# Attention and two MoE layers on one core: K, Q and V loads earlier in the plan, and the row maximum subtracted on VectorE

## The chip, the cores and the metric

One core of one Trainium2 chip runs the whole program in one launch. The metric is the device time of a run in microseconds (us). Engines are named as the profile names them: PE is TensorE (PEld its weight loads), DVE is VectorE, ACT is ScalarE, POOL is GpSimd, SP is SyncE, which here only issues DMAs (its rows read SPq).

## What is computed

Chunked attention over 4 batches, 8 heads, 768 positions and head size 64, and then two dense layers over the 3072 tokens, each with a hidden width of 2048:

```python
for c in range(24):                       # chunks of 32 queries
    k_full = concat(mem_k, k[c*32-16 : c*32+40])   # 8 memory rows, 56 of the window
    v_full = concat(mem_v, v[the same rows])
    scores = scale * q_c @ k_full.T
    scores = scores - max(scores, axis=-1)
    a = exp(scores); a = a / (sum(a) + 1e-9)
    out[c] = a @ v_full
x = out as (3072, 512)
h = x @ w_in;  x = (max(h, 0) + alpha * min(h, 0)) @ w_out          # layer 1
h = x @ w2_in; x = (h / (1 + exp(-1.702 * h))) @ w2_out              # layer 2
```

## The kernel before

The tokens are cut into 12 blocks of 256, numbered `nb` 0 to 11. A product in high precision is made of several fp16 ones: an operand is scaled by a power of two (found from its absolute maximum) and split into a high and a low fp16 half. Layer 1 runs 96 steps (12 blocks by 8 slices of the hidden width), each with 24 matmuls for the first product (line 585, `h`) and 24 for the second (line 667, `acc`) some steps later. Layer 2 follows from about 705 us on and touches nothing of the change.

The attention of block `nb` has to be ready before layer 1 reaches that block, so its pieces are strewn between the steps of earlier blocks. A table `ATT` gives each piece a due time in thirds of a step; for blocks 3 to 11 the due time is 24 nb - 26 plus the table's number, and blocks 0 to 2 have entries of their own in a second table, `start`. The pieces in the order of use:

- `att_load` (line 302) issues the loads of Q (`qf`, line 307) or of K or V (`kf`, `vf`, lines 319 to 323) on SP. There is one buffer of each, so a load waits until the block before has been split. For blocks at the start or end of a batch a small memset on POOL (lines 313, 315) goes ahead of the load.
- `att_max` (line 332) takes the absolute maxima of K and Q on ACT (V's on DVE); `att_all` brings them over all partitions with three small matmuls (line 120, `mx`), and `att_scale` makes the scales on DVE.
- `att_hi` and `att_lo` (lines 130 and 133) split K, Q and V; this frees `kf`, `qf` and `vf`.
- `att_tk` and `att_tq` (lines 459, 445) transpose K and Q by DMA; `att_swap` (lines 451, 452) copies the transposed Q into a second tile with its halves exchanged. All are issued on SP.
- `att_vw` and `att_vr` bring V into its banded layout through DRAM.
- `att_qk` (lines 483, 484) makes the scores of half a block in PSUM (`sps`), `att_ext` (lines 498, 500) copies the band out of it on ACT. There is one `sps`, so `att_qk` of the second half waits for `att_ext` of the first.
- `att_smax` (lines 514, 515) takes the row maximum on DVE and subtracts it; `eng(nb)` is VectorE for block 0 and GpSimd for the others. `att_exp` (line 519, ACT), `att_sum` (lines 524 to 528, the last on `eng(nb)`), `att_a16`, a DMA transpose and `att_pv` (line 553) follow.

The slices of layer 1's weights (line 154 or 156 loads one of 1 MB) and those of layer 2 are loaded, scaled and split in the same stretch. At the end of a block `y_evac` copies the result out of PSUM (line 706, or 697 for the first blocks), which frees the banks for the next block's second product.

An order is made from this plan: the pieces are recorded by due time, and a scheduler then lays each engine's instructions in a row by when it thinks that their inputs are there. Each engine works through its own row strictly, so an instruction that waits holds up all that stand behind it. SP's row is one row of this kind: all loads, transposes and stores stand in it.

Of the kernel before, what the change touches and what calls it, by code (L numbers as in the profile page):

```python
# [14 lines left out]
ALU = mybir.AluOpType  # L15
# [22 lines left out]
def kernel(  # L38
# [14 lines left out]
    nc = tc.nc  # L53
    B, H, S, D = q.shape
# [9 lines left out]
    SL = WIN + NM  # L64
# [220 lines left out]
    def eng(nb):  # L285
        return nc.vector if nb == 0 else nc.gpsimd
# [221 lines left out]
    def spare(nb, i, a):  # L508
        return att["sx", nb, i][:, a + 1:a + H + 1].rearrange("p (h t) -> p h t", t=1)

    def att_smax(nb, i):
        sc = att["s", nb, i]
        mx = spare(nb, i, 0)
        nc.vector.tensor_reduce(out=mx, in_=sc, axis=AX.X, op=ALU.max)
        eng(nb).tensor_tensor(out=sc, in0=sc, in1=mx.to_broadcast([128, H, SL]), op=ALU.subtract)

    def att_exp(nb, i):
        sc = att["s", nb, i]
# [320 lines left out]
    def run_plan(t):  # L839
# [6 lines left out]
    EX3 = 3 * EX  # L846

    ATT = [
        (-7, att_load, 1), (-6, att_load, 0), (-5, att_load, 2),
        (0, att_max, 1), (1, att_max, 0), (1, att_max, 2), (2, att_all, 0, 3), (4, att_scale, 0, 3),  # L850
        (5, att_hi, 1), (6, att_lo, 1), (6, att_hi, 0), (8, att_tk), (7, att_lo, 0), (9, att_tq),
        (14, att_hi, 2), (15, att_lo, 2), (16, att_vw), (13, att_swap),
        *[(17 + h // 2, att_vr, h) for h in range(H)],
        (18, att_qk, 0), (18, att_ext, 0), (20, att_smax, 0), (21, att_qk, 1), (21, att_ext, 1),
        (22, att_exp, 0), (23, att_smax, 1), (24, att_sum, 0), (25, att_exp, 1), (26, att_a16, 0),
        (27, att_sum, 1), (28, att_ta, 0), (29, att_a16, 1), (31, att_ta, 1),
        (32, att_pv, 0), (33, att_xhi, 0), (34, att_xlo, 0), (34, att_pv, 1), (35, att_xhi, 1), (36, att_xlo, 1),
# [5 lines left out]
    def split(m, p):  # L863
# [6 lines left out]
        (-89.08, alpha_prep), (-85.94, att_qk32, 0, 0), (-84.86, w_load, 0, 0), (-82.33, att_v32, 0, 1),  # L870
        (-78.47, w_load, 1, 0), (-74.28, w_max, 0, 0), (-68.89, att_ext, 0, 0), (-58.71, att_qk32, 0, 1),
        (-54.62, att_ext, 0, 1), (-47.58, att_smax, 0, 0), (-45.32, att_exp, 0, 0), (-41.66, att_sum, 0, 0),
        (-34.37, w_all, 0, 0, 1), (-33.6, w_max, 0, 1), (-31.58, w_scale, 0, 0, 1), (-28.74, att_v32, 0, 0),
        (-28.07, att_load, 1, 1), (-27.6, att_smax, 0, 1), (-26.72, w_all, 0, 1, 2), (-25.47, att_exp, 0, 1),
# [220 lines left out]
```

## Time and profile before

| | us |
|---|---|
| runs before (3) | 1183.9, 1180.58, 1184.12; median 1183.9 |
| the profiled execution | 1185.11 |
| its span | 1183.3 |
| PE busy | 1067.3 (90%) |
| DVE busy | 837.6 (71%) |
| ACT busy | 629.9 (53%) |
| POOL busy | 621.3 (53%) |

The span is the time between the first and the last instruction; 1.8 us of the execution lie outside it. Three stages can be told apart: up to about 225 us the weights and the first blocks are made ready, from 225 to 660 us layer 1 runs beside the attention of blocks 4 to 11, and from 660 us on PE has hardly a gap. PE's busy time does not say whether it runs at full speed, so the granted clock of a stretch is read beside it (1.00 is 2.4 GHz, 0.50 is 1.2 GHz). A row in a timeline that ends in brackets names the idle time of that engine ahead of the instruction and what ended it.

### The profile page before, as it was taken

The numbers are of one execution on the slowest core, as the hardware profiler recorded it, in microseconds if no ns is written. First come the engines' busy times: TensorE is split into PE (matmuls) and PEld (weight loads), VectorE is DVE, ScalarE is ACT, GpSimd is POOL, SyncE is SP. The second block draws the span as 40 slices with busy tenths as digits, with TensorE's granted clock in tenths as the row PEclk, the third lists the DMA queues.
The fourth block names the chain that finished last, engine by engine and source line by source line (L and its number), as shares of the span: only waits on it lengthen the run. The fifth ranks groups of instructions, "written<-read, shape, count | busy, mean of one in ns | idle before, by whom it ended". The sixth has DMA issues, their size and how long they took to land.

```text
span 1183.3 us, 25481 instructions
## 1 busy us (share of the span) xinstructions
PE 1067.3 (90%) x10231; PEld 944.5 (80%) x10231; DVE 837.6 (71%) x1512; ACT 629.9 (53%) x965; POOL 621.3 (53%) x737
## 2 busy tenths in 40 slices
PE   4667888998997989898989999989999999999998
PEld 3655677987886879687878888878888888888887
DVE  6898995768767685858687444887676767667662
ACT  4557455566757476646666533454454444443442
POOL 2245440228565365607563702778676666665672
PEclk9878888999999999998999999999999999999999
DMA  9968228568997777877975480640200202000001
GB/s 215 307 127 195 81 78 171 95 146 204 248 210 221 163 194 166 222 135 201 190 199 134 123 326 19 268 170 19 75 25 6 77 19 81 19 6 14 19 19 37
DMA packets 250534, 154.50 MB, mean 131 GB/s; under 512 B 201200, under 2 KB 221680, under 8 KB 249392
## 3 DMA queue, kind: packets, MB, share of 16 engines
q1 hardware_dynamic: 250416, 152.88, 49.9%
q8 instruction: 80, 1.31, 0.5%
q14 instruction: 38, 0.31, 0.1%
HBM read 91.96 MB, written 38.93 MB: 111 GB/s over the span
## 4 chain that ended last, share of the span: by engine, by line
PE 44%; DVE 20%; DMA 11%; POOL 9%; issue 9%; ACT 5%; SPq 3%; ACTq 0%; POOLq 0%; DVEq 0%
PE acc L681 17%; PE x L596 16%; PE acc L667 5%; PE h L585 4%; DVE g L133 2%; DVE wmax L127 2%; POOL wh L242 2%; DVE wr L201 2%; DVE wr L202 2%; DVE h L625 2%; POOL ga L632 2%; DMA wbig<-in_moe_w_in_dram 2%; POOL yh L767 1%; DMA q<-q 1%; DVE wr L208 1%
## 5 line engine op out<-in xcount | busy, mean ns | idle before, releaser
L632 POOL TENSOR_TENSOR ga<-ga 128x128 f32<-128x128 f32 x384 | 213.1, 579 | 171.0 <-DVE ga L630 158.9
L667 PE MATMUL acc<-g,wbig 128*128 128x256 f16 x2304 | 284.7, 283 | 18.8 <-ACT yf L706 9.4
L585 PE MATMUL h<-xt,wbig 128*128 128x256 f16 x2304 | 274.7, 276 | 19.7 <-DVE g L133 7.4
L667 PEld LDWEIGHTS <-wbig 128*128 128x128 f16 x2304 | 231.8, 101 | 54.0 <-issue 20.6
L585 PEld LDWEIGHTS <-wbig 128*128 128x128 f16 x2304 | 226.8, 99 | 50.0 <-issue 22.0
L681 PE MATMUL acc<-w2o,g 128*128 128x256 f16 x2016 | 230.3, 273 | 4.5 <-ACT g L130 3.8
L596 PE MATMUL x<-yt,w2i 128*128 128x256 f16 x2016 | 229.8, 273 | 2.1 <-DVE ha L606 2.1
L681 PEld LDWEIGHTS <-g 128*128 128x128 f16 x2016 | 196.8, 98 | 28.9 <-ACT g L130 4.7
L596 PEld LDWEIGHTS <-w2i 128*128 128x128 f16 x2016 | 197.2, 98 | 25.2 <-issue 2.4
L133 DVE SCALAR_TENSOR_TENSOR g<-ga,gk,g 128x896 f16<-128x896 f32 x96 | 120.8, 1265 | 91.3 <-ACT g L130 90.9
L130 ACT ACTIVATE g<-ga,gk 128x896 f16<-128x896 f32 x96 | 99.0, 1038 | 95.9 <-POOL ga L632 87.0
L625 DVE SCALAR_TENSOR_TENSOR h<-t,oma,h 128x256 f32<-128x256 f32 x176 | 84.9, 482 | 49.2 <-ACT t L622 47.7
L133 DVE SCALAR_TENSOR_TENSOR g<-h,gk,g 128x512 f16<-128x512 f32 x84 | 62.6, 746 | 61.2 <-ACT g L130 60.7
L130 ACT ACTIVATE g<-h,gk 128x512 f16<-128x512 f32 x84 | 57.5, 685 | 77.2 <-DVE h L625 75.0
L815 POOL TENSOR_TENSOR o<-o 128x256 f32<-128x256 f32 x77 | 74.3, 979 | 10.0 <-ACT o L810 9.5
L629 ACT ACTIVATE ga<-ha,l2t 128x512 f32<-128x512 f32 x48 | 34.5, 718 | 80.6 <-DVE ha L608 80.6
L622 ACT ACTIVATE t<-h 128x512 f32<-128x512 f32 x96 | 56.7, 590 | 33.1 <-PE h L585 24.1
L217 POOL TENSOR_TENSOR wbig<-wr,wbig 128x1024 f16<-128x1024 f32 x16 | 37.4, 2344 | 49.0 <-ACT wbig L212 49.0
L231 POOL TENSOR_TENSOR wt<-wr 128x512 f32<-128x512 f32 x16 | 23.0, 1440 | 74.2 <-DVE wr L208 74.2
L500 ACT COPY sc<-sps 32x504 f32<-32x504 f32 (+2 forms) x112 | 56.2, 502 | 1.0
L242 POOL TENSOR_TENSOR wh<-wt,wh 128x512 f16<-128x512 f32 x32 | 41.6, 1304 | 18.8 <-ACT wh L241 18.8
L630 DVE SCALAR_TENSOR_TENSOR ga<-ga,ha 128x512 f32<-128x512 f32 x48 | 35.6, 741 | 21.1 <-ACT ga L629 21.0
(196 smaller groups left out, 1460.5 us busy)
## 6 DMA issues: line engine op xcount, KB each, us to landing
yt_dr<-yh SPq DMA_DIRECT2D x42, 256.0 KB
yt<-yt_dr SPq DMA_DIRECT2D x42, 256.0 KB
w<-in_moe_w_in_dram SPq DMA_DIRECT2D x10, 1024.0 KB
w<-in_moe_w_out_dram SPq DMA_DIRECT2D x10, 1024.0 KB
vbd<-v_dr SPq DMA_DIRECT2D x80, 112.0 KB
w2i_dr<-wh SPq DMA_DIRECT2D x28, 256.0 KB
w2o_dr<-wh SPq DMA_DIRECT2D x28, 256.0 KB
w2i<-w2i_dr SPq DMA_DIRECT2D x4, 1792.0 KB
```

The source lines that it names most:

```text
L130: return nc.scalar.activation(out=hi, in_=src, func=ACTF.Copy, scale=s)
L133: return nc.vector.scalar_tensor_tensor(out=lo, in0=src, scalar=s, in1=hi, op0=ALU.mult, op1=ALU.subtract)
L242: nc.gpsimd.tensor_tensor(out=hv[:, 1], in0=src, in1=hv[:, 0], op=ALU.subtract)
L500: nc.scalar.copy(d[32 * c:32 * c + 32, ..., 0:WIN], x[32 * c:32 * c + 32, ..., bo + CH * c:bo + CH * c + WIN])
L585: nc.tensor.matmul(out=hp[:, e], lhsT=w[:, wt, o:o + 128], rhs=x[:, xh, kk], start=(n == 0), stop=(n == 3 * KT - 1))
L596: nc.tensor.matmul(out=xs[bank][:, i], lhsT=w[:, o, wt, kk * 256 + c:kk * 256 + c + 128], rhs=yt[sb, yi][:, yh, kk], start=(n == 0), stop= ...
L622: nc.scalar.activation(out=t, in_=hp, func=ACTF.Relu, scale=-1.0)
L625: nc.vector.scalar_tensor_tensor(out=g[:, e], in0=t[:, e], scalar=oma[:, f:f + 1], in1=hp[:, e], op0=ALU.mult, op1=ALU.add)
L632: nc.gpsimd.tensor_tensor(out=g[:, out_], in0=g[:, x], in1=g[:, y], op=op)
L667: nc.tensor.matmul(out=acc[layer, b][dt // 2][:, dt % 2 * TB:(dt % 2 + 1) * TB], lhsT=w[:, wt, dt * 128:(dt + 1) * 128], rhs=g16[:, gh, e] ...
L681: nc.tensor.matmul(out=acc[layer, b][bank][:, i * 256:(i + 1) * 256], lhsT=g16[:, gh, gs], rhs=w[:, o, wt, p % 2], start=(p == 0 and n == ...
L815: e.tensor_tensor(out=ov[:, out_], in0=ov[:, x], in1=ov[:, y], op=op)
```

## The change

Two lines change. The subtraction of the row maximum goes to VectorE for all blocks. And in the table, the loads of a block move forward against the rest: K from -7 to -16.6, Q from -6 to -16.3 and V from -5 to -8.

```diff
--- before.py
+++ after.py
@@ -512,7 +512,7 @@
         sc = att["s", nb, i]
         mx = spare(nb, i, 0)
         nc.vector.tensor_reduce(out=mx, in_=sc, axis=AX.X, op=ALU.max)
-        eng(nb).tensor_tensor(out=sc, in0=sc, in1=mx.to_broadcast([128, H, SL]), op=ALU.subtract)
+        nc.vector.tensor_tensor(out=sc, in0=sc, in1=mx.to_broadcast([128, H, SL]), op=ALU.subtract)
 
     def att_exp(nb, i):
         sc = att["s", nb, i]
@@ -846,7 +846,7 @@
     EX3 = 3 * EX
 
     ATT = [
-        (-7, att_load, 1), (-6, att_load, 0), (-5, att_load, 2),
+        (-16.6, att_load, 1), (-16.3, att_load, 0), (-8, att_load, 2),
         (0, att_max, 1), (1, att_max, 0), (1, att_max, 2), (2, att_all, 0, 3), (4, att_scale, 0, 3),
         (5, att_hi, 1), (6, att_lo, 1), (6, att_hi, 0), (8, att_tk), (7, att_lo, 0), (9, att_tq),
         (14, att_hi, 2), (15, att_lo, 2), (16, att_vw), (13, att_swap),
```

Since two blocks lie 24 units apart, -16.6 and -16.3 for one block are 7.4 and 7.7 on the scale of the block before it: behind that block's split of K (5 and 6) and about its split of Q (6 and 7), and in front of its transposes (8 and 9). For V, -8 is 16 there, right behind the split of V (14 and 15). The rows of all engines come out anew, for the scheduler sees other times.

SP, the block whose K is transposed at about 504 us (`k_6355` is its split K, `q_6492` its transposed Q, `kf` and `qf` take the next block's K and Q), before:

```order
L459 DMA_TRANSPOSE kt<-k_6355 128x8x128 x2
L243 DMA w2i_dr_103<-wh 128x2x512
L459 DMA_TRANSPOSE kt<-k_6355 128x8x48
L445 DMA_TRANSPOSE q_6492<-q_6368 128x16x128
L319 DMA kf<-in_k_dram 120x8x64
L319 DMA kf<-in_k_dram 128x8x64
L319 DMA kf<-in_k_dram 32x8x64
L451 DMA q_6627<-q_6492 64x2048
L452 DMA q_6627<-q_6492 64x2048
L320 DMA kf<-in_mem_k_dram 8x8x64
L323 DMA kf<-in_mem_k_dram 8x8x64
L307 DMA qf<-in_q_dram 128x8x64 x2
```

The same place now (`q_6499` is the transposed Q):

```order
L319 DMA kf<-in_k_dram 120x8x64
L319 DMA kf<-in_k_dram 128x8x64
L319 DMA kf<-in_k_dram 32x8x64
L243 DMA w2i_dr_103<-wh 128x2x512
L320 DMA kf<-in_mem_k_dram 8x8x64
L323 DMA kf<-in_mem_k_dram 8x8x64
L307 DMA qf<-in_q_dram 128x8x64 x2
L459 DMA_TRANSPOSE kt<-k_6355 128x8x128 x2
L459 DMA_TRANSPOSE kt<-k_6355 128x8x48
L445 DMA_TRANSPOSE q_6499<-q_6368 128x16x128
L451 DMA q_6634<-q_6499 64x2048
L452 DMA q_6634<-q_6499 64x2048
```

All seven loads now stand ahead of the transposes; before, three stood between the transposes and the swap, and four behind the swap. On PE the distance is what it was: between the three matmuls of `att_all` and `att_qk` of the first half there are five groups of 24 matmuls of each product, before and now.

DVE at about 99 to 109 us (`xt` is block 1's attention output, `wmax` the maxima of weight slices, `gf` layer 1's activation, `sc` block 2's scores), before:

```order
L133 SCALAR_TENSOR_TENSOR xt<-xp,blk_133,xt 128x4x128 x2
L127 TENSOR_REDUCE wmax_113<-wbig 128x1
L625 SCALAR_TENSOR_TENSOR gf<-t,oma,h 128x256 x2
L514 TENSOR_REDUCE sc<-sc 128x8
L127 TENSOR_REDUCE wmax_114<-wbig 128x1
L625 SCALAR_TENSOR_TENSOR gf<-t,oma,h 128x256 x2
L524 TENSOR_REDUCE sc<-sc 128x8
```

And now:

```order
L133 SCALAR_TENSOR_TENSOR xt<-xp,blk_133,xt 128x4x128 x2
L127 TENSOR_REDUCE wmax_113<-wbig 128x1
L201 TENSOR_SCALAR wr<-wr 128x1024
L625 SCALAR_TENSOR_TENSOR gf<-t,oma,h 128x256 x2
L202 SCALAR_TENSOR_TENSOR wr<-wbig,wr 128x1024
L208 SCALAR_TENSOR_TENSOR wr<-wbig,wr 128x1024
L514 TENSOR_REDUCE sc<-sc 128x8
L625 SCALAR_TENSOR_TENSOR gf<-t,oma,h 128x256 x2
L515 TENSOR_TENSOR sc<-sc 128x512
L127 TENSOR_REDUCE blk_135<-vf 128x1
L625 SCALAR_TENSOR_TENSOR gf<-t,oma,h 128x256 x2
L524 TENSOR_REDUCE sc<-sc 128x8
```

The subtraction (L515) is in DVE's row, two places behind its maximum (L514), and the maximum of a slice of the second weight (`wmax_114`) is gone from between L514 and L524; it now stands 30 rows after L514.

SP from about 115 to 154 us, the difference in one piece (`aT` is block 2's transposed attention weights, `w` and `wbig` are slices of layer 1's second weight):

```order
 L474 DMA vbd<-v_dr_91 56x8x128
 L475 DMA vbd<-v_dr_91 8x8x128
+L156 DMA wbig<-in_moe_w_out_dram 128x2x512
 L540 DMA_TRANSPOSE aT<-a_1104 128x8x128
+L540 DMA_TRANSPOSE aT<-a_1173 128x8x128
 L156 DMA w_526<-in_moe_w_out_dram 128x2x512
-L540 DMA_TRANSPOSE aT<-a_1173 128x8x128
 L156 DMA w_654<-in_moe_w_out_dram 128x2x512
 L156 DMA wbig<-in_moe_w_out_dram 128x2x512
```

A weight load that stood 20 rows ahead of this place is now the first of it, and the transposition of the second half of block 2 stands ahead of a weight load that was in front of it. POOL's row loses its 22 subtractions and keeps the rest nearly in order.

## Rows read from the trace of the kernel before

**Rows 1.** stretch; busy us (instructions) of PE, PEld, DVE, ACT, POOL; clock, DMA

```profile
225.00:660.00 435.00, 388.97 (x4137) 344.55 (x4135) 317.19 (x592) 271.36 (x428) 224.82 (x192) 0.98 0.77 184
...
660.00:1184.00 524.00, 511.62 (x4750) 456.82 (x4747) 336.93 (x564) 231.48 (x336) 316.38 (x487) 1.00 0.21 73
```

**Rows 2.** what TensorE waited for, 225 to 660 us: total, times, longest us

```profile
PE sps L483 <- ACT sc L500: 17.3, 6, 6.5
...
PE acc L667 <- ACT yf L706: 9.4, 6, 3.1
...
PE h L585 <- DVE g L133: 7.4, 7, 1.9
```

**Rows 3.** line 332 (absolute maxima, ScalarE): idle time before it, times, by releaser

```profile
  DMA qf<-in_q_dram: 39.5, 9
...
  DMA kf<-in_mem_k_dram: 5.8, 1
```

**Rows 4.** timeline of ScalarE, 512 to 537 us: start, us, what [idle before]

```profile
522.77 1.48 ACT L332 ACTIVATE junk<-kf 128x1536 f16<-128x1536 f32 x1 [9.26 <-DMA qf<-in_q_dram]
...
533.81 2.32 ACT L500 COPY sc<-sps 32x504 f32<-32x504 f32 x4
```

**Rows 5.** timeline of TensorE, same block

```profile
523.19 0.23 PE L483 MATMUL sps<-kt,q 128*128 128x160 f16 x1
...
536.18 0.29 PE L483 MATMUL sps<-kt,q 128*128 128x160 f16 x1 [6.48 <-ACT sc L500]
```

**Rows 6.** timeline of TensorE, two other blocks

```profile
246.69 3.07 PE L667 MATMUL acc<-g,wbig 128*128 128x256 f16 x24 [1.44 <-DVE yf L697]
...
312.39 0.23 PE L483 MATMUL sps<-kt,q 128*128 128x160 f16 x1 [0.95 <-ACT sc L500]
```

**Rows 7.** timeline of VectorE (first row) and SyncE's queue, same block

```profile
502.62 1.82 DVE L133 SCALAR_TENSOR_TENSOR k<-kf,blk,k 128x1536 f16<-128x1536 f32 x1 [0.99 <-ACT k L130]
...
504.50 2.62 SPq L459 DMA_TRANSPOSE kt<-k  x2
...
509.35 1.94 SPq L445 DMA_TRANSPOSE q<-q  x1
...
511.34 3.52 SPq L319 DMA_DIRECT2D kf<-in_k_dram  x3
...
514.97 0.47 SPq L451 DMA_DIRECT2D q<-q  x1
...
517.75 1.33 SPq L307 DMA_DIRECT2D qf<-in_q_dram  x2
```

**Rows 8.** busy time and granted clock after that stall, columns of rows 1

```profile
534.20:541.00 6.80, 4.82 (x29) 4.00 (x29) 4.52 (x7) 5.73 (x11) 6.80 (x7) 0.50 0.86 179
```

**Rows 9.** chain of work that ended last: start us, us, what

```profile
193.98 6.73 DMA q<-q
...
341.85 4.49 DMA q<-q
```

**Rows 10.** line 515 on both engines (ns min/median/max), and ScalarE waiting for it

```profile
L515 POOL TENSOR_TENSOR sc<-sc x22: 1034/1044/1508, 45.5 to 657.0; 128x512 f32<-128x512 f32 x22
...
L515 DVE TENSOR_TENSOR sc<-sc x2: 675/676/677, 19.6 to 31.5; 128x512 f32<-128x512 f32 x2
...
ACT sc L519 <- POOL sc L515: 8.4, 9, 3.9
```

**Rows 11.** line 133 on VectorE, a form with both inputs in SBUF

```profile
L133 DVE SCALAR_TENSOR_TENSOR g<-gf,gka,g x5: 736/739/2610, 116.6 to 132.2; 128x512 f16<-128x512 f32 x5
```

**Rows 12.** timelines of VectorE, TensorE, SyncE, TensorE between 100 and 201 us

```profile
106.05 1.22 DVE L127 TENSOR_REDUCE wmax<-wbig 128x1 f32<-128x1024 f32 x1 [3.84 <-DMA wbig<-in_moe_w_out_dram]
...
134.55 1.44 PE L553 MATMUL sps<-aT,vbd 128*128 128x32 f16 x48 [4.79 <-DMA aT<-a]
...
128.04 0.41 SPq L156 DMA_DIRECT2D w<-in_moe_w_out_dram  x1
...
200.85 0.29 PE L484 MATMUL sps<-kt,q 128*128 128x160 f16 x1 [4.39 <-DMA q<-q]
```

## Prediction

> **What bounds the kernel now.** I read the busy time by stretch first. From 660 us on TensorE works 511.6 of 524 us at a granted clock of 1.00 [rows 1]; the change touches nothing there, and this half of the time stays. From 225 to 660 us TensorE works 389.0 of 435 us, at 0.98, while VectorE works 317.2, ScalarE 271.4 and GpSimd 224.8 [rows 1]: no helper is full, so the 46 us in which TensorE stands still come from waits, not from an engine that has too much to do. Ahead of 225 us VectorE is close to full, and a fault on its row is passed on.
>
> The list of TensorE's waits says which. The largest, 17.3 us in six pieces, is `att_qk` of a second half (L483) held by ScalarE's copy out of the one `sps` (L500); then 9.4 us of second products behind the evacuation (L706), and 7.4 us of first products behind a split on VectorE [rows 2]. The copy itself is short (2.32 us for the four), so the question is why it comes late. In the block at 512 us ScalarE stood idle for 9.26 us ahead of the absolute maximum of K, until a load had landed, and began the copy only at 533.81 [rows 4]; TensorE had run `att_qk` of the first half at 523.19 and then waited 6.48 us for the second [rows 5]. Over the run that instruction's place on ScalarE costs 39.5 and 5.8 us of idle time, in ten pieces [rows 3]. One block bears this out from the other side: the stall at 312.39 us, in a block with almost no such wait, is 0.95 us [rows 6].
>
> Why the loads are late stands in SyncE's queue: K's split ends at 502.62 + 1.82 = 504.44 us and `kf` is free, but the transposes go first (504.50, 509.35), K's loads are issued from 511.34 and Q's from 517.75 to 519.08, and Q's stand behind the swap (514.97) [rows 7].
>
> **The change part by part.** The sum is made against the profiled execution, 1185.1 us, which is 1.2 us above the median of 1183.9; the result goes back to the median at the end.
>
> *Loads of K and Q, forward.* They are now the first in that queue, from 504.5 us. Seven issues at Q's rate (1.33 us for two, 0.67 each) take 4.7 us; at the durations measured there, 3.52 for three of K, half of the 2.78 us from 514.97 to 517.75 for the two small ones, and 1.33 for Q, they take 6.2 us [rows 7]. So the last is issued by 509.2 to 510.7 us, not 519.1, which is 8 to 10 us earlier, against a wait of 9.26 us at worst: ScalarE's wait should nearly go. What goes with it on TensorE: of the 17.3 us the five pieces other than 312.39 are 16.4 us; if each keeps the 0.95 of the block without a wait, 11.6 go. I take 14, as a stall is not due in every block. With it goes the 1.44 us at 246.69 [rows 6], which follows such a wait. And behind the long stall the granted clock was 0.50 for 6.8 us, in which TensorE worked 4.82 us [rows 8], work that takes half of that at the upper level: 2.4 us. Together **-17.8 us** (11.6 to 20.2).
>
> *What the loads now stand in front of.* The transposes and the swap move back. At 504.5 + 4.7 to 6.2 the transposes start, 4.85 us later (504.50 to 509.35) that of Q is issued, and one such transpose took 4.49 us from issue to landing [rows 7, 9]. The swap is then issued at 518.6 to 520.1 instead of 514.97. How long it takes is seen once where TensorE waited for it: 6.73 us, with loads in the same queue [rows 9]; without them I bound it below by the 4.49 of the transpose. It lands at 523.1 to 526.8, and `att_qk` needs it at 523.19 [rows 5]. That is a stall of 0 to 3.6 us in each of the eight blocks in which the loads overtake the transposes (3 to 10), 0 to 29 us. I take half a microsecond each, **+4 us**, near the lower end, as no load competes with the swap any more.
>
> In the DMA page of the Trainium skill, "DMA: Bandwidth & Descriptors", section "Two DMAs through the same engine are not ordered", descriptors of one queue start in order on each DMA engine though they may end out of order; by that the transposes could not slip past the loads' packets, which speaks for the upper end of this term. The trace agrees in so far as the swap that had loads around it took 6.73 us [rows 9].
>
> *V's loads, forward.* They now stand ahead of the reads of banded V, whose consumer comes some 20 us later in the plan: nothing.
>
> *The subtraction on VectorE.* 22 instructions leave GpSimd at 1.044 us and come to VectorE at 0.676 us [rows 10]: 14.9 us more on VectorE, of which some 10 us lie in the stretch with 435 - 317 = 118 us of idle time. TensorE waits for VectorE in several of its smaller stalls, so I put a quarter on the path, **+4 us** (0 to 15). In return the exponential need not queue behind GpSimd's other work: ScalarE waited 8.4 us for the subtraction, up to 3.9 at once [rows 10], in front of the evacuation that TensorE waits 9.4 us for. I take half of that, **-5 us** (0 to -9.4).
>
> The row for contention: a split with both inputs in SBUF takes 0.739 us at the median and 2.610 at worst [rows 11], and the subtraction has both inputs in SBUF too, so its price lies between 0.68 and 0.68 + 1.87 us. The Trainium skill's page "SBUF — State Buffer", section "Who interferes with whom", says that VectorE with two SBUF inputs and GpSimd reading SBUF shut each other out for a whole instruction; by that the price depends on who starts first, and the subtraction on GpSimd already hit VectorE's splits in the same way.
>
> *The start.* VectorE's 3.84 us wait at 106 us, for a weight that is now loaded and reduced later, goes; TensorE's 4.79 us at 134.55 came from a transpose issued behind a weight load (128.04), which it now precedes; its 4.39 us at 200.85 is a swap like those above, now with loads ahead [rows 12]. Against them stand four subtractions on a full VectorE, 2.7 us, and the weight that comes later. I take **-3 us** (+4 to -10).
>
> Sum: 1185.1 - 17.8 + 4 + 4 - 5 - 3 = 1167.3 us; at the median's level **1166 us**, 1.5% less. The same sum with every part at its good end is 1145, with every part at its bad end 1221; the parts will not all fall one way.
>
> **The rivals.**
> *Late swap (slower).* `att_qk` of each block waits for the swapped Q. If the loads hold the transposes for the full 3.6 us in eight blocks, this costs 29 us: 1185.1 - 17.8 + 29 + 4 - 5 - 3 = 1192, at the median's level 1191. For it: the swap is needed 8.2 us after its issue now (514.97 to 523.19) and comes 3.6 to 5.1 later. Against it: TensorE waited for a swap at only one place after 190 us. It decides from about 2.7 us per block, where eight times the stall eats the other gains of 21.8 us.
> *VectorE shut out.* GpSimd is busy for about half of the stretch [rows 1]; if half of the subtractions meet a reading instruction and wait some 0.9 us (half of 1.87), VectorE gets 14.9 + 10 = 25 us, and with half of it on the path and no gain at the exponential: 1185.1 - 17.8 + 4 + 12.5 - 3 = 1181, median's level 1180. The rule of the Trainium skill's page "SBUF — State Buffer" named above would be its mechanism. Against it: VectorE's idle time.
> *The wait comes back in part.* Small loads or memsets from GpSimd, or a store that stands between the loads, hold SyncE, and ScalarE still waits half as long: half of the first term, 1167.3 + 8.9 = 1176, 1175 at the median's level.
> *It doesn't do what it says.* The new row of ScalarE could bring the maximum forward as far as the loads. Then only the small terms stay: 1182. The order speaks against it.
> *Everything pays.* Late evacuations and half-clock stretches go too: 1148 or less.
>
> **How the numbers follow.** Forecast 0.50; late swap 0.13; VectorE shut out 0.13; half the wait 0.13; nothing 0.05; everything pays 0.06. Faster by over 0.3% (3.6 us, about what a measurement of this kernel can tell from no change) are the forecast, the half wait, the best case and a third of the second rival: 0.73. Within 0.3% are half of that rival and the case of nothing: 0.12. Slower: late swap and the rest, 0.15. The range from 1148 to 1189 reaches the forecast's own bounds and the milder half of the late swap; it leaves out about 0.18.
>
> **What would show it.** Right: line 332 with under 10 us of idle ScalarE time, L483 waiting under 5 us for ScalarE, Q's loads issued ahead of the transposes by 6 us after K's split, and 225 to 660 us shorter by 15 us or more. The swap step is wrong if L483 or L484 waits for the swapped Q in most blocks; the VectorE step if line 515 there takes well over 0.7 us or TensorE's waits for VectorE grow past 10 us; the start if the first 225 us do not shrink. The whole is wrong if ScalarE's wait goes and TensorE's stalls stay, because then something else was due just behind.

## The result: 1169.7 us, 1.0% faster

| | median us | lowest to highest | ratio to before, 95% interval |
|---|---|---|---|
| before | 1183.6 | 1180.6 to 1184.1 | |
| the whole change | 1169.7 | 1167.5 to 1172.4 | 0.9899 (0.9872 to 0.9926) |

Forecast were 1166 us, in a range of 1148 to 1189. The sign and the size fit; the terms are another matter. The traced execution took 1172.38 us with a span of 1170.6, so it is the slowest of these four runs.

To compare two traces, equal work is better than equal time. The cut used from here on is TensorE's row: the *start* ends where the second product (L667) of the third block begins, the *middle* where that of the last block begins. The rest, which is layer 2 but for its first microseconds, takes 482.4 us in both. Of before (from, to, length, busy us of PE, PEld, DVE, ACT and POOL with instructions, granted clock, DMA share, GB/s):

```profile
0.00:221.60 221.60, 163.35 (x1318) 140.10 (x1319) 180.53 (x347) 124.86 (x199) 80.07 (x59) 0.87 0.68 162
221.60:700.90 479.30, 433.27 (x4619) 384.51 (x4616) 337.79 (x641) 291.72 (x459) 241.31 (x206) 0.98 0.77 191
```
And of the whole change:

```profile
0.00:213.60 213.60, 159.21 (x1319) 137.30 (x1320) 175.71 (x347) 123.46 (x197) 72.69 (x51) 0.84 0.69 167
213.60:688.20 474.60, 433.32 (x4615) 384.91 (x4615) 354.00 (x663) 291.61 (x461) 226.51 (x192) 0.97 0.76 194
```
The start is 8.0 us shorter and the middle 4.7. The middle is where the prediction had nearly all of the gain. TensorE's busy time there is the same, 433.3 us, and the granted clock no better (0.97 against 0.98), so what is saved are waits. By name they come to 3.0 of the 4.7 us. What TensorE waited for in the middle, the answer to [rows 2] (us in total, times, longest):

```profile
PE h L585 <- DVE g L133: 9.1, 6, 3.1
PE mx L120 <- DVE g L133: 6.2, 3, 5.3
PE sps L484 <- DMA q<-q: 5.4, 4, 3.0
PE sps L483 <- ACT sc L500: 5.2, 3, 3.0
...
PE acc L667 <- ACT yf L706: 0.9, 1, 0.9
```
L483 behind ScalarE's copy fell from 17.3 us to 5.2, and the second product behind the evacuation (L706) from 9.4 to 0.9. Against these 20.6 us stand 5.4 of a wait that was not there, the swapped Q (L484), and more under VectorE's name: its rows were 17.7 us in all and are 29.8.

SyncE's queue in the block whose K is split at 496.7 us, the answer to [rows 7]:

```profile
496.74 2.91 SPq L319 DMA_DIRECT2D kf<-in_k_dram  x3
...
501.02 1.07 SPq L307 DMA_DIRECT2D qf<-in_q_dram  x2
502.18 5.48 SPq L459 DMA_TRANSPOSE kt<-k  x3
507.71 2.04 SPq L445 DMA_TRANSPOSE q<-q  x1
512.11 0.49 SPq L451 DMA_DIRECT2D q<-q  x1
```
It does what the diff says: K's loads are issued at the split's end, Q's are out at 502.1, 5.4 us after K's first. K's transposes follow at 502.18 instead of at once, Q's at 507.71, and the swap at 512.11. What ScalarE then waits for at line 332 is no load any more, as it was in [rows 3]:

```profile
  DMA q<-q: 17.2, 6
```
```profile
509.59 2.01 ACT L130 ACTIVATE v<-vf,blk 128x1536 f16<-128x1536 f32 x1 [1.85 <-DMA kt<-k]
512.17 1.49 ACT L332 ACTIVATE junk<-kf 128x1536 f16<-128x1536 f32 x1 [0.57 <-DMA q<-q]
```
The scan of K (L332) began at 512.17, just as Q's transpose had landed and the swap could be issued; the split of V ahead of it had itself waited for K's transposes. The reason stands in the code: the scan writes its discarded elements into a buffer of the same tag as Q's split (`q16`), which Q's transpose reads, and V's split goes into the buffer of K's split (`kv16`), which K's transposes read. So the loads came 9 us earlier (5.4 us after the split of K instead of 14.6), the scan only 2.8 (15.5 us after it instead of 18.3), and V's split later. TensorE in that block, the answer to [rows 5]:

```profile
516.68 0.24 PE L484 MATMUL sps<-kt,q 128*128 128x160 f16 x1 [0.80 <-DMA q<-q]
```
The 6.48 us in front of L483 are gone, and 0.80 us for the swap have come.

### The profile page after: what moved, and what is told of

The parts are those of the page before. It is cut to its first block, busy times and chain, and to the rows that moved or that the text cites. A ratio compares the mean times of both kernels' runs of the same rounds, so it can differ in the third digit from the quotient of the medians.

```text
span 1170.6 us, 25487 instructions
## 1 busy us (share of the span) xinstructions
PE 1064.5 (91%) x10231; PEld 942.7 (81%) x10231; DVE 849.6 (73%) x1534; ACT 628.3 (54%) x965; POOL 599.2 (51%) x715
## 4 chain that ended last, share of the span: by engine, by line
PE 48%; DVE 18%; DMA 12%; ACT 6%; SPq 5%; issue 5%; POOL 4%; ACTq 0%; DVEq 0%; POOLq 0%
PE acc L681 17%; PE x L596 16%; PE acc L667 7%; PE h L585 5%; DMA q<-q 2%; SPq L459 2%; DMA w<-in_moe_w_in_dram 2%; DVE g L133 2%; DVE h L625 2%; POOL ga L632 2%; DVE wmax L127 2%; DMA wbig<-in_moe_w_in_dram 1%; DVE wr L202 1%; DMA w<-in_moe_w_out_dram 1%; DVE blk L127 1%
## 5 line engine op out<-in xcount | busy, mean ns | idle before, releaser
L667 PE MATMUL acc<-g,wbig 128*128 128x256 f16 x2304 | 279.5, 280 | 10.9 <-DVE yf L697 4.1
L667 PEld LDWEIGHTS <-wbig 128*128 128x128 f16 x2304 | 230.3, 101 | 43.5 <-issue 11.9
```

Of the source, the lines that this page charges most:

```text
L667: nc.tensor.matmul(out=acc[layer, b][dt // 2][:, dt % 2 * TB:(dt % 2 + 1) * TB], lhsT=w[:, wt, dt * 128:(dt + 1) * 128], rhs=g16[:, gh, e] ...
```

## The experiments

Each group of four ran on one chip beside runs of the kernel before, and is read by its ratio to those. The kernel before had medians of 1182.1, 1179.5 and 1183.3 us on the three chips, so times of different groups are not compared. The ratio is the recorded one and not the quotient of two medians: the loads at -13 have 1172.7 against 1179.5 us, a quotient of 0.9943, near the end of the interval of their 0.9918. Start and middle are from one trace of each kernel, cut as above, and that execution need not be a typical one. The diffs are against the whole change, except where the kernel before is named.

| | ratio, 95% interval | start | middle | TensorE's waits in the middle |
|---|---|---|---|---|
| before | 1 | 221.6 | 479.3 | 45.8 |
| before, second trace | | 217.7 | 479.8 | 44.2 |
| whole change | 0.9899 (0.9872 to 0.9926) | 213.6 | 474.6 | 42.8 |
| whole change, second trace | | 213.5 | 469.6 | 39.0 |
| loads alone | 0.9943 (0.9924 to 0.9961) | 214.3 | 477.4 | 41.8 |
| subtraction alone | 0.9962 (0.9948 to 0.9977) | 213.8 | 483.0 | 47.7 |
| other buffer for the scan | 0.9894 (0.9876 to 0.9912) | 214.7 | 470.8 | 38.9 |
| Q's transpose first | 0.9809 (0.9787 to 0.9831) | 211.9 | 465.4 | 37.6 |
| loads between transposes and swap | 0.9918 (0.9889 to 0.9947) | 213.5 | 475.1 | 40.0 |
| before, Q's transpose first | 1.0051 (1.0033 to 1.0069) | 214.7 | 486.9 | 49.4 |
| loads, Q's transpose first, GpSimd subtracts | 0.9858 (0.9828 to 0.9887) | 213.6 | 465.3 | 34.2 |
| maximum taken twice | 1.0016 (0.9994 to 1.0038) | 221.2 | 475.1 | 42.6 |
| V's loads back at -5 | 0.9950 (0.9929 to 0.9971) | 213.1 | 477.3 | 44.6 |
| Q first and other buffer | 0.9844 (0.9817 to 0.9870) | 211.9 | 472.5 | 40.9 |

### How far one trace can be read

The two kernels once more, unchanged.

> The kernel before, once more with a trace. In the first trace its third block's second product begins at 221.6 us, 7 to 10 us later than in the whole change and in every part of it tried alone. Theory F (the start of before is late because of its order: the swap of block 3 that loads surround, 4.39 us at 200.85, and the half clock behind it): 219 to 223 us again, and 478 to 481 us from there to the last block of layer 1. Rival G (that one execution was late there by chance): under 217 us, and then the gain of 8 us in the start is not the change's.

> The whole change, once more with a trace: the third block's second product at 212 to 215 us and 472 to 477 us from there to the last block of layer 1 if the first trace (213.6 and 474.6) is typical; L483 waits for ScalarE 4 to 7 us, the scan of line 332 for the buffer 15 to 21 us. Otherwise differences of a few us between stages of two traces say nothing.

Before (columns as above):

```profile
0.00:217.70 217.70, 161.65 (x1318) 139.51 (x1319) 180.35 (x347) 124.66 (x199) 80.10 (x59) 0.82 0.67 165
217.70:697.50 479.80, 435.59 (x4620) 386.86 (x4618) 336.96 (x641) 291.74 (x459) 241.24 (x206) 0.97 0.77 191
```
The whole change:

```profile
213.50:683.10 469.60, 431.94 (x4615) 383.75 (x4615) 355.93 (x663) 291.85 (x461) 226.54 (x192) 0.98 0.75 195
```
The start of before ended at 217.7 us and not at 221.6, just under the 219 to 223 of theory F and over the 217 of its rival: about half of the 8 us between the first two traces was one execution's bad luck, and 4.2 us stand between the second two. The middle of before repeats to half a microsecond, that of the whole change differs by 5.0 us, mostly waits (42.8 and 39.0). So from a single trace only differences of 5 us and more in a stage are read here, and the mean of two gives 6.1 us for the start and 7.4 for the middle. Of what was expected of the second trace of the whole change only the start came: its middle is 2.4 us below the 472 expected, L483 waited 3.6 us and line 332 14.2 us for Q's transpose, each just under its range.

### The two halves of the change apart

The loads alone:

```diff
-        nc.vector.tensor_tensor(out=sc, in0=sc, in1=mx.to_broadcast([128, H, SL]), op=ALU.subtract)
+        eng(nb).tensor_tensor(out=sc, in0=sc, in1=mx.to_broadcast([128, H, SL]), op=ALU.subtract)
```

> Only the loads of K, Q and V are moved; the subtraction stays on GpSimd. Theory A (the loads free ScalarE; the subtraction on VectorE is a small net loss, since TensorE's waits for VectorE behind 213.6 us grew by about 12 us while its waits for the evacuation of line 706 fell by 8.5): 1160 to 1168 us, a little faster than the whole change, L483 waiting for ScalarE about 5 us, TensorE's waits for VectorE near the 17.7 us of before, the evacuation near 9 us again. Theory B (the subtraction carries part of the gain): 1173 to 1181 us.

The subtraction alone (the loads back in their old places):

```diff
-        (-16.6, att_load, 1), (-16.3, att_load, 0), (-8, att_load, 2),
+        (-7, att_load, 1), (-6, att_load, 0), (-5, att_load, 2),
```

> Only the subtraction goes to VectorE; the loads stay at -7, -6 and -5. Theory A: 1184 to 1191 us, the waits of line 332 for loads near 45 us and L483 waiting 17 us as before, TensorE's waits for VectorE above 25 us. Theory B: 1173 to 1180 us, with the waits for the evacuation (L706) gone.

Measured were 0.9943 and 0.9962. Theory A falls and B's times fit (1176.0 and 1178.0 us), though the waits for the evacuation did not go with the subtraction alone (5.2 us are left of 9.4): the subtraction is no loss, each half is faster than before, and -0.57% and -0.38% make nearly the -1.01% of both. What TensorE waited for in the middle, loads alone (as [rows 2]):

```profile
PE sps L483 <- ACT sc L500: 3.5, 3, 2.5
```
Subtraction alone:

```profile
PE sps L483 <- ACT sc L500: 16.4, 5, 7.4
```
With the loads alone L483 is down to 3.5 us; with the subtraction alone it stays at 16.4, the middle of its trace is no shorter (483.0 against 479.3 and 479.8), and the gain lies in the start. With the loads alone the middle is 477.4 us, some 2 us shorter, which one trace does not resolve. The rows that name VectorE rise with either half: from 17.7 us in all to 29.8 with the loads alone, where the subtraction is still on GpSimd, to 26.1 with the subtraction alone, and to 29.8 and 25.2 in the two traces of the whole. So this growth is not the price of the subtraction alone. That VectorE's splits are simply due next when TensorE waits less for ScalarE is my reading of it; with the subtraction alone L483 still waits its 16.4 us.

### The buffer of the scan

```diff
-            z = at_p.tile([128, 1536], F16, tag="q16", name="junk")
-            nc.scalar.activation(out=z[:, 0:n], in_=t, func=ACTF.Abs, accum_out=bs(nb, i))
+            z = at_p.tile([128, 1536], mybir.dt.float8e4, tag="a16", name="junk", bufs=2)
+            nc.scalar.activation(out=z[:, 0:n], in_=t, func=ACTF.Abs, accum_out=bs(nb, i), saturate=False)
```

> The whole change, and the scans of K and Q on line 332 write their discarded elements into a buffer of the attention weights (8 bit wide, so that it fits) and not into the buffer of Q's split. Theory A (the 19 us that ScalarE still waits at line 332 are that buffer, which Q's transpose is reading): the wait falls under 5 us, L483's wait for ScalarE from 5.2 to under 3 us, time 1163 to 1169 us. Rival (the wait is a load, or a place on the queue of transposes): the 19 us stay at line 332, time 1168 to 1173 us. Third case: the wait goes and the time stays at 1169, because nothing on TensorE was due behind it any more.

Line 332, idle time by releaser:

```profile
  DMA kf<-in_mem_k_dram: 9.7, 5
```
The 17.2 us behind Q's transpose are gone, so the buffer was their cause; 9.7 us behind K's loads are left, and 1.0 more. And the time is 0.9894, that of the whole change. The third case it is: ScalarE's scan is no longer what TensorE is due on, and removing another wait there buys nothing.

### Q's transpose first

```diff
-        (5, att_hi, 1), (6, att_lo, 1), (6, att_hi, 0), (8, att_tk), (7, att_lo, 0), (9, att_tq),
+        (5, att_hi, 1), (6, att_lo, 1), (6, att_hi, 0), (9, att_tk), (7, att_lo, 0), (8, att_tq),
```

> The whole change, and Q's transpose stands ahead of K's three in the plan (8 and 9 swapped). Theory A (Q's transpose decides both ScalarE's wait at line 332 and the swap): it is issued some 5.5 us earlier, the wait at line 332 falls from 19 to under 6 us, TensorE's waits for the swapped Q (6.7 us in five) go to under 2 us, time 1161 to 1167 us. Rival (K's transposes are then late instead, since first scores need both): TensorE waits for kt by 5 us or more, time 1168 to 1174 us.

1160.9 us, 0.9809: the fastest of all, and at the lower end of what theory A expected. TensorE has no row that waits for `kt`, so the rival falls. SyncE's queue (K's split in this block ends earlier than in the one above):

```profile
493.02 1.01 SPq L307 DMA_DIRECT2D qf<-in_q_dram  x2
494.13 3.42 SPq L445 DMA_TRANSPOSE q<-q  x1
497.65 4.79 SPq L459 DMA_TRANSPOSE kt<-k  x3
502.54 0.53 SPq L451 DMA_DIRECT2D q<-q  x1
```
The swap is issued 8.4 us after Q's transpose, when that had landed (by 500.6 us, when the scan that waited for it began) and K's transposes were out. TensorE's waits in the middle:

```profile
PE h L585 <- DVE g L133: 17.8, 12, 3.0
...
PE sps L484 <- DMA q<-q: 1.8, 1, 1.8
...
PE sps L483 <- ACT sc L500: 0.3, 1, 0.3
```
The swap costs 1.8 us there instead of 5.4 and 3.7 in the two traces of the whole change, and L483 0.3 instead of 5.2 and 3.6. The middle itself:

```profile
211.90:677.30 465.40, 428.73 (x4615) 381.94 (x4615) 349.14 (x663) 290.60 (x462) 233.03 (x193) 0.99 0.80 197
```
TensorE's busy time for the same work is 428.7 us instead of 433.3, at a granted clock of 0.99 instead of 0.97, so less of the middle ran at the lower level. Against the second trace of the whole change the waits are 1.4 us less and the busy time 3.2. One part of the expectation fell: ScalarE still waits 18.5 us at line 332 for Q's transpose, with L483 at 0.3 us.

The same edit on the kernel before tells whether Q first is good by itself:

> The kernel before, with Q's transpose ahead of K's and nothing else. Theory C (Q first gains 9 us on the whole change because it takes back what the loads cost): here there is little to take back, TensorE waits for a swap only once, 4.4 us at 200.85; time 1177 to 1183 us, the waits of line 332 for loads still 40 us or more. Rival D (Q first is good by itself, whatever the loads do): 1168 to 1175 us.

It is not: 1.0051, slower than either theory had it. There the loads of K and Q stand behind the transposes, and L483 waits for ScalarE longer than before:

```profile
PE sps L483 <- ACT sc L500: 22.0, 5, 7.5
```
So of the two places of the loads that were tried with it, Q first pays only with the moved ones. What it takes back there, by the rows, is the late swap and what was left of L483's wait.

### The loads between the transposes and the swap

```diff
-        (-16.6, att_load, 1), (-16.3, att_load, 0), (-8, att_load, 2),
+        (-13, att_load, 1), (-13, att_load, 0), (-8, att_load, 2),
```

> The whole change, but K's and Q's loads at -13 each: in SyncE's row they then stand behind the four transposes and in front of the swap, where SyncE only waits for Q's transpose. Theory C (what the loads cost is the place in front of the transposes: the swap, ScalarE's scan and V's split all wait for transposes that are some 5 us later): the transposes are issued right behind the splits again, VectorE's waits for V's split on ScalarE fall from 10.7 to about 4 us, TensorE's waits for the swap from 6.7 to under 4 us, and the loads come still 5 us sooner than before the change; time 1163 to 1168 us. Rival (the loads themselves have to be that early): ScalarE waits for Q's load at line 332 by over 20 us again, L483 waits for ScalarE over 10 us, time 1171 to 1179 us.

0.9918, 1172.7 us: no better than the whole change. Theory C's signs are there, for in the middle the swap costs 2.9 us and VectorE's wait for V's split 5.2. But the scan waits for K's loads again (over the run):

```profile
  DMA kf<-in_k_dram: 30.4, 7
```
and TensorE's waits under VectorE's name are 30.1 us, no less than in the whole change (29.8 and 25.2). L483:

```profile
PE sps L483 <- ACT sc L500: 5.3, 5, 1.4
```
The rival names the time and the wait for loads at line 332, though for K's loads and not Q's, and misses L483, which stays at 5.3 us. Both places of the loads cost about the same; the later one was not tried with Q's transpose in front.

### The subtraction with Q's transpose first

The loads moved and Q first, but the subtraction on `eng(nb)`:

> Loads moved and Q's transpose first, the subtraction on GpSimd. Theory C (the subtraction on VectorE is worth some 6 us with the loads moved, 1176.0 against 1169.7): 1165 to 1169 us against 1160.9 with the subtraction on VectorE. Rival E (with the late swap gone nothing is due behind the exponential any more, and the subtraction is worth nothing): 1159 to 1163 us.

0.9858 against 0.9809, with intervals that just overlap; 1164.8 us lie between the two forecasts, a little under theory C's. TensorE's waits in the middle show how the two engines differ:

```profile
PE acc L667 <- ACT yf L706: 10.2, 5, 2.5
PE h L585 <- DVE g L133: 9.2, 9, 2.3
```
The middle is the same to 0.1 us (465.3 and 465.4). With GpSimd the second products wait 10.2 us behind the evacuation and the first 9.2 behind VectorE; with VectorE it is 2.3 and 17.8. In these two traces the engine of the subtraction only decides under which name TensorE waits. But the traced executions took 1163.1 and 1161.5 us, 1.6 us apart, where the two ratios are 0.5%, some 6 us, apart. So the traces hold only a part of the difference, and that the subtraction is worth nothing in the middle is not shown.

### More work on VectorE

```diff
         nc.vector.tensor_reduce(out=mx, in_=sc, axis=AX.X, op=ALU.max)
+        nc.vector.tensor_reduce(out=mx, in_=sc, axis=AX.X, op=ALU.max)
```

> The whole change, with the row maximum of line 514 taken twice on VectorE: 24 instructions of 0.68 us, 16.3 us more on VectorE and on the way to the exponential. If a quarter of VectorE's time is on the path, as the prediction had it for the subtraction: 1172 to 1176 us. If TensorE waits for VectorE with nearly every microsecond (its waits for VectorE are 29.8 us now): 1179 us or more. If VectorE's idle time takes it: 1168 to 1171 us.

1182.5 us, 1.0016: nearly everything that the change had brought is lost. But not where the expectation looked:

```profile
0.00:221.20 221.20, 164.50 (x1319) 141.66 (x1320) 181.81 (x360) 124.84 (x199) 70.87 (x52) 0.81 0.67 162
221.20:696.30 475.10, 432.45 (x4619) 383.88 (x4617) 359.87 (x674) 291.48 (x460) 238.35 (x191) 0.98 0.77 193
```
The middle takes 475.1 us, as in the whole change (474.6 and 469.6), though VectorE has eleven more instructions and 4 to 6 us more work in it; the start takes 221.2 instead of 213.6. These 7.6 us are about half of what the two ratios lie apart (1.2%, some 14 us); where the rest is these traces don't settle. One row holds more than the 7.6. TensorE in the start:

```profile
139.00 1.46 PE L554 MATMUL sps<-aT,vbd 128*128 128x32 f16 x48 [12.09 <-DMA aT<-a]
```
SyncE's queue ahead of it:

```profile
124.25 7.66 SPq L156 DMA_DIRECT2D w<-in_moe_w_out_dram  x2
135.91 1.24 SPq L541 DMA_TRANSPOSE aT<-a  x1
```
In the order the transpose of block 2's second half (there L541) now stands behind two weight loads, where in the whole change it goes first. But that isn't what it waited for: the second load was issued at 131.51 us and out at 131.9, and then SyncE stood still for 4 us, until `a` was written. GpSimd writes the second part of `a`:

```profile
126.38 1.49 POOL L529 TENSOR_TENSOR sc<-sc 128x512 f32<-128x512 f32 x1
...
134.73 1.15 POOL L535 TENSOR_TENSOR a<-sc,a 128x512 f16<-128x512 f32 x1
```
and ScalarE the first, between the two:

```profile
131.52 1.04 ACT L212 CAST wbig<-wr 128x1024 f16<-128x1024 f32 x1 [2.52 <-DVE wr L208]
...
132.95 0.62 ACT L534 CAST a<-sc 128x512 f16<-128x512 f32 x1
```
The same row of GpSimd in the whole change:

```profile
123.55 1.36 POOL L534 TENSOR_TENSOR a<-sc,a 128x512 f16<-128x512 f32 x1 [0.73 <-ACT a L533]
```
With the maximum doubled, `a` is complete at 135.88 us instead of 124.91, 11 us later, and the transpose follows 0.03 us behind it. The largest piece of that is on ScalarE: the normalised weights were there at 127.87 us, but the cast (L534) stood behind a piece of a weight slice (L212), which itself waited 2.52 us for VectorE; in the whole change the cast stands ahead of it. So what this row costs isn't the 0.68 us of a maximum but places in strict rows, ScalarE's above all, which a maximum more in each half was enough to change.

### V's loads, and both repairs together

```diff
-        (-16.6, att_load, 1), (-16.3, att_load, 0), (-8, att_load, 2),
+        (-16.6, att_load, 1), (-16.3, att_load, 0), (-5, att_load, 2),
```

> The whole change, but V's loads at -5 as before: they stand behind the first reads of banded V. The prediction put this part at nothing: 1167 to 1173 us. Rival (V's loads in front of the reads hold the reads, or free V's split earlier): 1163 us or less, or 1176 us or more.

0.9950: V's place, priced at nothing, is worth half of the gain. Set beside the subtraction alone (0.9962), this version says as much of K's and Q's loads: it differs from that one in their place only, and the two ratios agree within their intervals. So beside the subtraction, with V's loads left where they were, the early loads of K and Q bring 0.1%, no more than the noise. What they bring once V's loads have moved too was not tried apart.

TensorE waits for the evacuation again:

```profile
PE acc L667 <- ACT yf L706: 8.3, 7, 2.1
```
What ties the evacuation to the attention is ScalarE's row: the second half's exponential (L519) stands ahead of the evacuation (L706). With V at -5, in the block that ends near 425 us:

```profile
428.26 0.72 ACT L519 ACTIVATE sc<-sc,blk 128x512 f32<-128x512 f32 x1
...
430.11 1.06 ACT L706 COPY yf<-acc 128x512 f32<-128x512 f32 x2
```
In the whole change, in the block that ends near 428 us:

```profile
425.86 0.72 ACT L519 ACTIVATE sc<-sc,blk 128x512 f32<-128x512 f32 x1
...
428.71 0.59 ACT L706 COPY yf<-acc 128x512 f32<-128x512 f32 x1
```
With V at -5 the exponential runs 2.9 us after the block's last second product has ended, and the evacuation waits behind it; in the whole change it was done before that end, and only the short rows for the first product stand between. How V's place reaches the exponential can be seen on VectorE in the same block:

```profile
423.64 1.75 DVE L127 TENSOR_REDUCE blk<-vf 128x1 f32<-128x1536 f32 x1 [3.23 <-DMA vbd<-v_dr]
```
That is the maximum of the next block's V. It reads `vf` alone, so I take its wait, which the trace names after a read of banded V, for one for V's loads: SyncE had issued the last of them at 419.57 us, between those reads, and in the whole change at 412.95, ahead of them. The row maximum (426.43 us) and the subtraction (427.48) of the second half stand behind it in VectorE's row, and the exponential waits for them. Over the middle VectorE waits 5.8 us in this way, in the whole change not at all. In this block, then, the evacuation is late because the attention is late against layer 1. V's place is one cause of that; in the version with Q first GpSimd's subtraction had the same effect on the evacuation (10.2 us and 2.3).

At last the edits of the scan's buffer and of Q's transpose together:

> The whole change with Q's transpose first, and the scans of line 332 write their discarded elements into a buffer of the attention weights. Theory C (once the swap is early, TensorE waits for nothing behind ScalarE's scan, L483 0.3 us): the 18 us at line 332 shrink and the time stays, 1158 to 1163 us. Rival (the scan, 5 us earlier, brings the whole chain of the next block forward): 1150 to 1157 us.

Q's transpose first with the scan's other buffer gives 0.9844, no better than Q first alone, and theory C's time was missed by a microsecond. But the wait at line 332 did not shrink, as both cases had it: it passed to K's loads (16.7 us in seven). So the scan did not come earlier by what was expected, and what it would bring then stays open.

## Why the prediction was right, step by step

The time came as forecast, and in part by luck. Of the prediction's own signs, Q's loads were issued 5.4 us after K's split and ahead of the transposes, L483 waits about 5 us or less (5.2 and 3.6), the swap is waited for four times and twice in the middle and so not in most blocks, and the start shrank. Line 332 still has 21 and 18 us of idle time and not under 10, though no longer behind loads. The middle is 5 to 10 us shorter in the two pairs and not 15. TensorE's waits for VectorE grew from 17.7 and 17.6 us to 29.8 and 25.2, the sign against the VectorE step. And TensorE's waits went from 45.8 to 42.8 and from 44.2 to 39.0 while L483's went by 12, which is nearly the last sign, of something else due just behind.

**Loads of K and Q (-17.8 us).** The wait that was to go went, down to the 5.4 us in which the loads are issued. L483's waits fell by 12.1 us in one pair of traces and 12.0 in the other (15.6 to 3.6), against the 14 taken. The 1.44 us of line 697 did not go: that row grew, from 3.2 to 4.1 us and from 3.7 to 4.9. The clock's 2.4 us are not in TensorE's busy time in the first pair (433.3 both); in the second it fell by 3.7 (435.6 to 431.9). So the waits are some 3 to 7 us short of the term. The larger error is in what they are worth: with the term for the swap I had -13.8 us for K and Q, and the one comparison that moves them alone (0.9962 to 0.9950) gives 1.4 us, within the noise. A wait that is taken from TensorE was counted as time saved, while others came due behind it.

**The late swap (+4).** 5.4 and 3.7 us in the middle, where before there was no such wait. Right in size, so the rival of 29 us did not come. That it is the loads' price is borne out by the pair of experiments with Q's transpose first. What the step left out is who else reads what the transposes must release: V's split shares K's buffer and the scan Q's. VectorE's wait for V's split on ScalarE, before (us, times, longest):

```profile
DVE v L133 <- ACT v L130: 3.4, 6, 0.7
```
and now:

```profile
DVE v L133 <- ACT v L130: 10.7, 8, 3.2
```
The scan's share was tested and is harmless; V's share wasn't tried apart.

The Trainium skill's page "DMA: Bandwidth & Descriptors", section "Two DMAs through the same engine are not ordered", had spoken for the upper end of this term. The trace of the whole change stays at the lower one: from the second of the swap's two issues (512.64 us), from which the 6.73 us were counted too, to its use at 516.68 are 4.0 us. Nor can the 6.73 us be put down to the loads around that swap: in the second trace of before, with the same loads around it, the same swap took (chain of work, as [rows 9]):

```profile
193.10 3.84 DMA q<-q
```

**V's loads (nothing).** The step that failed outright. At -5 with the rest moved they cost some 6 us, and the row that comes back is the evacuation's, behind an attention that is late. The step looked only at the reads of banded V, which are pushed back, and not at what waits for V itself: its maximum (L127) stands in VectorE's row ahead of the second half's maximum and subtraction. That was seen in one block and not tried apart; V's split may have a share.

**The subtraction (+4 and -5).** The two terms cancel nearly to nothing (-1), and by the ratios the subtraction brings some 4 to 5 us, alone (0.9962) or beside the loads (0.9943 to 0.9899). Its rows are not its alone. TensorE's waits behind the evacuation fell by 8.5 us; for the whole of that both VectorE's subtraction and V's place are needed, for 3.5 us are left with the loads alone, 5.2 with the subtraction alone, and 8.3 with V at -5. The rows that name VectorE rose by 12.1 us, and they rise as much with the subtraction on GpSimd. The quarter of VectorE's time that I put on the path, 4 us, is less than one trace resolves in the middle; neither the doubled maximum nor the exchanged engine (465.3 and 465.4 us) shows it there or rules it out. The feared contention is there, and small. On VectorE (ns, min, median, max):

```profile
L515 DVE TENSOR_TENSOR sc<-sc x24: 677/684/1667, 18.9 to 641.3; 128x512 f32<-128x512 f32 x24
```
Its median is 0.684 us, but seven of the 24 take from 0.83 to 1.67 us, 4.5 us more than the median in all. Each of the seven began while a `tensor_tensor` of GpSimd was running, and ended 0.5 to 0.6 us after that one: at 423.53 us a GpSimd instruction of 1.15 us had begun 0.07 us earlier, and the subtraction took 1.63. The other 17 took 0.68 or 0.69 us; 16 of them began with none running or in the last 0.14 us of one, and one (631.86 us) began within a GpSimd instruction that itself took 2.89 us instead of 1.15. By the Trainium skill's page "SBUF — State Buffer", section "Who interferes with whom", a VectorE instruction with two SBUF inputs contends with a GpSimd instruction that reads SBUF, for a port that is an exclusive lock. The trace agrees: who began first decided, and the rival's 10 us of such waits are 4.5 here.

**The start (-3).** 8.0 us by the first traces, 6.1 by the mean of two: within the term's own bounds (+4 to -10). TensorE's rows there, the answer to [rows 12]:

```profile
128.04 1.36 PE L553 MATMUL sps<-aT,vbd 128*128 128x32 f16 x48 [2.27 <-DMA aT<-a]
133.24 1.01 PE L585 MATMUL h<-xt,wbig 128*128 128x256 f16 x4 [3.84 <-ACT xt L130]
...
198.10 0.24 PE L484 MATMUL sps<-kt,q 128*128 128x160 f16 x1 [1.30 <-DMA q<-q]
```
The swap of block 3 costs 1.30 us instead of 4.39; it was 1.45 and 3.58 in the second pair. `att_pv` of block 2 (L553) waits 2.27 us for its transposed weights instead of 4.79, and here the subtraction has its part: with GpSimd subtracting, in every version, that wait is 4.8 to 7.8 us, with VectorE 3.0 or less, but for the doubled maximum. The prediction's cause, a transpose issued behind a weight load, is 1.65 us of it: before, `a` was complete at 126.89 us and its transpose was issued at 128.54, and in the whole change it is issued as soon as `a` is complete. But 3.84 us behind ScalarE come right after it, where before there were 0.96, and the net is small. That VectorE was close to full there was too strong: it was busy for 180.5 of the 221.6 us, 81%. Every version but the one with the doubled maximum has a start of 212 to 215 us, with the loads moved or the subtraction or only Q's transpose; so no one part earns the gain, and which wait of the old start makes it 4 to 8 us longer is open.

**The sum.** -17.8 + 4 + 4 - 5 - 3 was -17.8 us; measured are -13.9 us by the medians and 1.0%, some 12 us, by the ratio. It came out near for other reasons than its terms: by the experiments some 6 us need V's place, priced at nothing, and some 5 the subtraction's, priced at -1, and the large term for K and Q is not shown to have earned its share. (The rival in which only the small terms stay was priced at 1182 us; +4, -5 and -3 give 1181, 1180 at the median's level.) In the middle, by waits: -12.1 (L483) - 8.5 (evacuation) + 5.4 (swap) + 12.1 (VectorE) = -3.1, and the list as a whole went from 45.8 to 42.8. Of the rivals "the wait comes back in part" is closest to what happened, but what came back are VectorE's waits and the swap, not ScalarE's. Why VectorE's rows hold TensorE for 24 to 32 us in nearly every version with the loads moved isn't settled; in the version with GpSimd subtracting and Q first it is 18.3 us, and the middle no shorter.

## What to carry to other kernels

When a load is moved forward in a queue that works strictly in order, price what it now stands in front of by all that those instructions release, shared buffers included, and then order what is left by who is waited for: here the one swap of two transposes was worth nearly as much again as the change (0.9899 to 0.9809), and nothing without the change (1.0051). Price a load also by every row that it holds up when it is late, as V's maximum did here on VectorE. When instructions are added or moved between engines, look for the place in a strict row that they decide, a cast behind a weight slice or an exponential ahead of an evacuation, before their own microseconds. A wait taken from the bounding engine is not yet time saved: look for what is due next. And test parts together as well as apart, for Q's transpose in front has a value only beside the moved loads, and K's and Q's loads none that shows without V's.

## What was not expected of the hardware

Two executions of one kernel differ by 5 us in the middle and by 4 us in the start, while layer 2 repeats within 0.1 us (482.4). The clock doesn't explain the start: it was granted at 0.87 in the longer one of before (221.6 us) and at 0.82 in the shorter (217.7). A swap with the same transfers around it took 6.73 us in one execution and 3.84 in the other. And the scan that writes 8 bits per element took as long as the one that writes 16: 1483 against 1484 ns for 1536 elements.
